# One paired DMA transpose split in two, and one exponential moved by a step, in a fused attention and feed-forward kernel on one core

## The chip, the cores and the metric

The kernel runs on 1 core of one Trainium2 chip. The metric is device time of one execution in microseconds (us), the median of several runs. TensorE (PE) multiplies matrices, VectorE (DVE), ScalarE (ACT) and GpSimd (POOL) work on elements, SyncE (SP) issues most DMAs.

## The reference

For each of 8 batches and 8 heads, 512 tokens `x` (width 64) and 32 states attend to each other; the 544 rows of every batch, 512 wide, then go through a feed-forward layer of width 2048 with a leaky ReLU.

```python
scores = scale * x @ state.T;   a  = softmax(scores);   xread = a @ state      # 512 rows per head
scores2 = scale * state @ x.T;  a2 = softmax(scores2);  sread = a2 @ x         # 32 rows per head
rows = concat([xread, sread])          # (8*544, 512) after the heads are joined
h = rows @ w_in;  g = maximum(0.01 * h, h);  out = g @ w_out
```

## The kernel before, in words

The batches run one behind the other. Each is an object `a` (`a0`, `a1`, `a2`, then `att_of[b]`), and its attention is prepared while the feed-forward of the batch before it keeps TensorE busy. The order of the instructions on every engine is the order in which the program writes them; engines wait for each other by semaphores alone.

The feed-forward of a batch is a loop of 16 steps `s`. Step `s` calls `ff1(a, hT, s)`: two matmuls into a PSUM bank `ph` (L428; there are two such banks, used in turn) and, on ScalarE, the leaky ReLU from that bank into `hT` (L433). Between the `ff1` of two steps stand products of the second layer (`piece`, `product`, `two_product`; tiles `py`, `ppx`, `ppb`, `ppr`) of this batch and of the one before, and the steps of the next batch's attention:

- `a_scores` (L256) fills the bank `sc` with scores of 32 states by 512 tokens, from `xT`, the tokens transposed by DMA (`a_xt_dma`, L234). `xT` comes from `xb`, the tokens cast by GpSimd (L132), and these from `xl`, loaded by SP (`load_x`, L99).
- `a_max`, `a_diff`, `a_exp` (ScalarE, L284), `a_recip`, `a_probs` give the first probabilities `aT`.
- `a_max2`, then `a_exp2(a, g)` for the two halves g = 0, 1 (ScalarE, L337, reading `sc`), then `a_probs2` (DVE, L345 to L355) give the second probabilities.
- The second probabilities are transposed by a DMA from SP: one by one (`a_a2t`, L362, of tile `a2`) for batches 2 to 5, in pairs (`a_a2t_pair`, L369, of tile `a2p`, which holds two batches) for batches 0 and 1 and for 6 and 7.
- `a_sread` (L380, PSUM tile `psr`, bank `big`) multiplies the transposed ones with `xb`; ScalarE copies the result to `sr_t` (L387). Its end also frees batch b's `xb` for a later batch.
- `a_m` (L407, tile `pm`) multiplies the states with `w_in` into `M`, a quarter at a time. At step 10 three of them stand in a row: into banks `ph` and `py` ("phpy"), into `big` and into `sc`.

The change touches two places. In the loop of batch 1 (L1053 to L1089), SP gets, in this order, `a_xt_dma` of batch 3 (step 7), `load_x(4)` (step 11), `a_a2t_pair(0)` (step 13), and then `a_a2t` of batch 2. In batch 2's loop `a_sread(a0)` stands in step 4 and `a_sread(a1)` in step 7, and batch 3's attention has `a_exp` in step 4, `a_exp2` in steps 6 and 8 (6 and 7 in later batches), and `a_probs` and `a_probs2` in step 8, with `a_m` in step 10.

Of the kernel before, what the change touches and what calls it, by code (L numbers as in the profile page):

```python
# [9 lines left out]
P = 128  # L10
# [5 lines left out]
NT = S // P  # L16
# [3 lines left out]
BF16 = mybir.dt.bfloat16  # L20
# [7 lines left out]
def kernel(  # L28
# [14 lines left out]
    att = ctx.enter_context(tc.tile_pool(name="att", bufs=2))  # L43
# [278 lines left out]
    def a_recip(a):  # L322
        a.q1b = block_recip(a.e1, NB)
# [18 lines left out]
    pairs = {}  # L342

    def a_probs2(a):
        nc.vector.tensor_scalar(out=a.r2[:], in0=a.r2[:], scalar1=1e-9, scalar2=None, op0=ALU.add)  # L345
        q2 = att.tile([P, 2], FP32, name="qc", tag="qc")
        nc.vector.reciprocal(q2[:], a.r2[:])
        if a.b in (0, 6):
            pairs[a.b] = att.tile([P, 2, 2, S], BF16, name="a2p", tag="a2p", bufs=1)
        if a.b in (0, 1, 6, 7):  # L350
            a.a2 = pairs[a.b - a.b % 2][:, a.b % 2]
        else:
            a.a2 = att.tile([P, 2, S], BF16, name="a2", tag="a2", bufs=1)[:]
        for g in range(2):
            nc.vector.tensor_scalar(  # L355
                out=a.a2[:, g, :], in0=a.e2[:, g, :],
                scalar1=q2[:, g:g + 1], scalar2=None, op0=ALU.mult,
            )
# [5 lines left out]
        )  # L364
        a.a2T = t[:]

    def a_a2t_pair(b):
        t = att.tile([P, 2, 2, NT, P], BF16, name="a2pT", tag="a2pT", bufs=1)
        nc.sync.dma_start_transpose(  # L369
            t[:].rearrange("p b g i q -> p (b g i) q"),  # L370
            pairs[b][:].rearrange("p b g s -> p (b g s)"),
        )
        for v in range(2):
            att_of[b + v].a2T = t[:, v]

    def a_sread(a):
        ps = psum.tile([P, NK, 2, NS], FP32, name="psr", tag="big", bufs=1)
# [379 lines left out]
    att_of = [Attn() for _ in range(B)]  # L757
# [148 lines left out]
    q = [recip0(0)]  # L906
# [62 lines left out]
    for j, tag in ((4, "ph"), (6, "big"), (8, "py"), (10, "big"), (12, "py"), (14, "ph")):  # L969
        t, bk = open_ff1_0(tag)  # L970
# [82 lines left out]
    for s in range(16):  # L1053
        ff1(a1, h1, s)
        if s % 2:
            pb, hT, i, jq = fill[s // 2]
            piece(pb, hT, i, jq)
        if s == 1:
            for n, j in ((3, 0), (3, 4), (4, 0)):
                tw_sum(n, j, j + 4, nc.vector)  # L1060
        elif s == 3:
            a_scores(a2)
            m_evict(a2, 0, a_m(a2, 0, "big"), SCA)
            a_shift(a2)
            a_max2(a2)
            tw_sum(4, 4, 8, nc.vector)
        elif s == 5:
            load_state(1)
        elif s == 7:
            a_exp(a2)  # L1070
            a_open(att_of[3], 3)
            a_xt_dma(att_of[3])
        elif s in (9, 11):
            a_exp2(a2, s // 2 - 4)
            if s == 9:
                a_recip(a2)
                a_probs(a2)
            else:
                a_probs2(a2)
                load_x(4, nc.sync)  # L1080
        elif s == 13:
            a_probs2(a1)
            a_a2t_pair(0)
            pm = [a_m(a2, 1, "big"), a_m(a2, 2, "sc")]
            m_evict(a2, 1, pm[0], VEC)
            m_evict(a2, 2, pm[1], SCA)
            q1 = two_open(h1, 2 * P, ("S0", "S1"), "py")
            for n in (1, 2, 3):
                two_sum(q1, n, 0, 4, nc.vector)  # L1089
# [3 lines left out]
    for b in range(2, B):  # L1093
        hT = hpool.tile([P, 16, S], BF16, name="hT", tag="hT")
        hTs[b] = hT
        a = att_of[b]
        nxt = att_of[b + 1] if b + 1 < B else None
        if b == 2:
            two_keep(q1, "S2")
            fill = {i: [lambda i=i: piece(1, h1, i, 3)] for i in range(2)}  # L1100
            for s, n in zip((2, 3, 5, 6, 8, 9, 11), (1, 2, 6, 5, 3, 7, 4)):
                fill[s] = [lambda n=n: two_product(q1, n)]
            fill[11].append(lambda: nc.sync.dma_start(pair_rows(1, 1), q1.y[:]))
        else:
            order = (2, 6, 5, 7, 3, 4)
            fill = {
                s: [lambda n=order[s // 2], v=s % 2: product(b - 1, n, v)] for s in range(12)
            }
            for i, n in enumerate(order):
                if n not in (2, 7):  # L1110
                    fill[2 * i + 1].append(lambda n=n: after(b - 1, n))
        fill[12 if b < 6 else 13] = [lambda: product(b, 1, 0)]
        fill[14] = [lambda: product(b, 1, 1, 0, 4)]
        fill[15] = [lambda: product(b, 1, 1, 4, 8), lambda: after(b, 1)]
        for s in range(16):
            ff1(a, hT, s)
            if s == 0:
                if b + 2 < B:
                    open_xb(b + 2)
                if b == 7:  # L1120
                    a_a2t_pair(6)
                elif b != 6:
                    a_a2t(a)
                for n in (1, 2) if b > 2 else (1, 2, 3):
                    if b > 2:
                        s_sum(b - 1, n, 4, 8, nc.vector)
                    else:
                        two_sum(q1, n, 4, 8, nc.vector)
            elif s == 1:
                if nxt is not None:  # L1130
                    a_scores(nxt)
                m_evict(a, 3, a_m(a, 3, "big"), SCA)
                if nxt is not None:
                    a_max(nxt)
                if b > 2:
                    for j in range(0, HJ, 2):
                        s_sum(b - 1, 4, j, j + 2, nc.gpsimd)
                else:
                    for j in (4, 0):
                        two_sum(q1, 4, j, j + 4, nc.gpsimd)  # L1140
                    state_cast(1, nc.gpsimd)
                if b + 2 < B:
                    cast_all(b + 2)
            elif s == 4:
                if b == 2:
                    state_t(1)
                    a_sread(a0)
            elif s == 7:
                if b == 2:
                    a_sread(a1)  # L1150
            elif s == 13:
                if b < 6:
                    a_sread(a)
            elif s == 10:
                if b == 7:
                    a_sread(att_of[6])
            elif s == 12:
                if b == 7:
                    a_sread(a)
                for n in (1, 2):  # L1160
                    s_sum(b, n, 0, 4, nc.vector)
                for j in (0, 4):
                    s_sum(b, 3, j, j + 4, nc.vector)
            if nxt is not None:
                if s == 4:
                    a_exp(nxt)
                elif s in ((6, 8) if b == 2 else (6, 7)):
                    if b == 2 and s == 6:
                        for f in fill.pop(6):
                            f()  # L1170
                    a_exp2(nxt, int(s > 6))
                if s == 7:
                    a_recip(nxt)
            if s == 9 and b + 2 < B:
                a_open(att_of[b + 2], b + 2)
                a_xt_dma(att_of[b + 2])
                if b + 3 < B:
                    load_x(b + 3, nc.sync)
            if b == 7:
                if s == 0:  # L1180
                    fa_open()
                elif s == 13:
                    fb_sums()
            for f in fill.get(s, ()):
                f()
            if b == 7 and s in FA_AT:
                i = FA_AT.index(s)
                fa_sum(i % 4 + 1, FJ * (i // 4), FJ * (i // 4 + 1))
            if s == 1:
                if b > 2:  # L1190
                    after(b - 1, 2)
                if nxt is not None:
                    a_diff(nxt)
                    if b > 2:
                        a_max2(nxt)
            elif s == 3 and b == 2:
                a_max2(nxt)
            elif s == (8 if b == 2 else 7):
                if b > 2:
                    after(b - 1, 7)  # L1200
                if nxt is not None:
                    a_probs(nxt)
                    a_probs2(nxt)
            elif s == 10 and nxt is not None:
                pm2 = a_m(nxt, 2, "phpy")
                pm0 = a_m(nxt, 0, "big")
                pm1 = a_m(nxt, 1, "sc")
                for g, copy in enumerate((SCA, VEC)):
                    copy(nxt.M[:, g, 2 * DM:3 * DM], pm2[g][:])
                m_evict(nxt, 0, pm0, VEC)  # L1210
                m_evict(nxt, 1, pm1, SCA)
# [3 lines left out]
    b = B - 1  # L1215
# [72 lines left out]
```

## Time and profile before

| | |
|---|---|
| time, median of 3 runs | 204.12 us (203.95 to 204.6) |
| the profiled execution's own time | 204.44 us |
| its span | 202.7 us |
| granted TensorE clock, mean | 0.998 |
| PE, DVE, ACT, POOL busy | 97%, 79%, 71%, 31% |

The profile is one execution, taken by the hardware profiler. Times in it count from the start of its span. L380 is line 380 of the kernel before. A row of a timeline gives the start, the time until the end of the last instruction that it joins, engine, line, operation, `out<-in`, sizes and count, and in brackets idle time before it with what ended it. "SPq" is SP's queue of issues: the time there is that of the issue, not of the transfer. In a list of waits the numbers are us in total, times, and the longest.

### The profile page before, as it was taken

The page shows a single profiled execution, that of the slowest core. Times are in us where ns is not written, and L with a number is a line of the kernel's source. Part 1 is how long each engine was busy: PE and PEld are TensorE (multiplying, and loading weights), DVE is VectorE, ACT ScalarE, POOL GpSimd, SP SyncE. Part 2 cuts the span into 40 slices and gives each one's busy share as a digit, 9 for nine tenths or more (in the row PEclk, how much of TensorE's full clock was granted, in tenths as well). Part 3 has the DMA queues.
Part 4 walks back from the last instruction along what each step waited for, and adds up shares of the span by engine and source line. Part 5 has one row for each costly group of instructions (what it writes and reads, how often), then busy time and mean ns, then how long its engine had stood idle before and what let it go on. Part 6 is the DMA issues. An engine that isn't in the chain of part 4 may idle for free.

```text
span 202.7 us, 4607 instructions
## 1 busy us (share of the span) xinstructions
PE 196.1 (97%) x1880; PEld 129.2 (64%) x1880; DVE 160.2 (79%) x242; ACT 144.3 (71%) x273; POOL 62.3 (31%) x67
## 2 busy tenths in 40 slices
PE   7979999999999999999999999999999999999993
PEld 2643534443467667766776677676767677799982
DVE  2865898899989999879996998699879935984712
ACT  3669777788979877778787779686958665757420
POOL 8734180030280274007600580054005600540000
PEclk9999999999999999999999999999999999999999
DMA  6999999697997726834194505220026202210115
GB/s 205 204 207 299 253 259 162 150 335 139 270 212 133 282 53 53 248 155 120 22 244 152 158 3 105 105 107 0 0 107 158 49 3 91 119 42 13 52 40 169
DMA packets 38741, 27.75 MB, mean 137 GB/s; under 512 B 24384, under 2 KB 35776, under 8 KB 38720
## 3 DMA queue, kind: packets, MB, share of 16 engines
q1 hardware_dynamic: 33552, 20.78, 40.3%
q0 software_dynamic: 4832, 6.29, 15.2%
q10 hardware_dynamic: 336, 0.39, 0.8%
q8 instruction: 14, 0.23, 0.5%
q14 instruction: 7, 0.06, 0.1%
HBM read 17.30 MB, written 8.91 MB: 129 GB/s over the span
## 4 chain that ended last, share of the span: by engine, by line
PE 76%; DMA 9%; DVE 7%; ACT 4%; POOL 1%; issue 1%; ACTq 1%; POOLq 0%
PE ph L428 18%; PE ppx L628 17%; PE ppb L628 15%; DMA w_in_bf<-in_moe_w_in_dram 5%; PE pyw L533 3%; PE ppr L685 3%; PE pm L407 3%; DMA a2pT<-a2p 3%; PE pf L506 3%; PE py L533 3%; PE ppw L628 3%; PE ph L933 2%; PE psr L380 2%; PE php L933 1%; DVE tw L572 1%; ACT hT L433 1%
## 5 line engine op out<-in xcount | busy, mean ns | idle before, releaser
L433 ACT ACTIVATE hT<-ph 128x512 bf16<-128x512 f32 x112 | 66.4, 603 | 24.0 <-PE ph L428 23.1
L428 PE MATMUL ph<-aT,M 128*128 128x512 bf16 x224 | 65.4, 380 | 0.1
L593 POOL TENSOR_TENSOR S<-hT,S 128x512 bf16<-128x512 bf16 x24 | 32.1, 1358 | 83.6 <-DVE S L593 65.5
L628 PEld LDWEIGHTS <-S 128*128 128x128 bf16 x384 | 37.3, 98 | 12.8
L628 PEld LDWEIGHTS <-hT 128*128 128x128 bf16 x288 | 27.6, 98 | 11.8 <-issue 1.9
L593 DVE TENSOR_TENSOR S<-hT 128x1024 bf16<-128x1024 bf16 x24 | 25.0, 1068 | 2.7 <-ACT hT L433 2.7
L428 PEld LDWEIGHTS <-M 128*128 128x128 bf16 x224 | 20.8, 98 | 9.5 <-issue 3.7
L628 PE MATMUL ppx<-tw,S 128*128 128x256 bf16 x160 | 20.7, 273 | 0.0
L533 PEld LDWEIGHTS <-hT 128*128 128x128 bf16 x96 | 9.0, 98 | 11.5 <-issue 1.3
L533 PE MATMUL py<-w_out_bf,hT 128*128 128x512 bf16 x64 | 16.0, 380 | 0.0
L421 ACT CAST M<-pm 128x1024 bf16<-128x1024 f32 x13 | 13.2, 1014 | 0.6 <-PE pm L407 0.6
L132 POOL CAST xb<-xl 128x2048 bf16<-128x2048 f32 x5 | 9.5, 1891 | 13.3 <-DMA xl<-in_x_dram 12.6
L725 DVE TENSOR_TENSOR ysb<-ppb,s 128x512 f32<-128x512 f32 x12 | 8.3, 692 | 5.5 <-PE ppb L628 5.5
L628 PE MATMUL ppb<-w_out_bf,hT 128*128 128x256 bf16 x96 | 12.5, 273 | 0.0
L628 PE MATMUL ppb<-tw,S 128*128 128x256 bf16 x96 | 12.4, 273 | 0.0
L628 PE MATMUL ppb<-w_out_bf,S 128*128 128x256 bf16 x96 | 12.3, 273 | 0.0
L628 PE MATMUL ppx<-w_out_bf,hT 128*128 128x256 bf16 x80 | 11.2, 273 | 0.0
L337 ACT ACTIVATE e<-sc,mcol 128x512 bf16<-128x512 f32 x16 | 11.1, 697 | 0.0
L289 DVE TRANSPOSE_TENSOR_REDUCE r<-e 128x32 f32<-128x1024 bf16 x7 | 8.7, 1245 | 2.9 <-ACT e L284 2.9
L628 PE MATMUL ppx<-tw,hT 128*128 128x256 bf16 x80 | 10.4, 273 | 0.0
L331 DVE TENSOR_REDUCE mcol<-sc 128x2 f32<-128x1024 f32 x8 | 9.7, 1214 | 0.0
L266 DVE TRANSPOSE_TENSOR_REDUCE mrow<-sc 128x32 f32<-128x1024 f32 x7 | 8.7, 1243 | 0.5 <-PE sc L256 0.5
(148 smaller groups left out, 311.5 us busy)
## 6 DMA issues: line engine op xcount, KB each, us to landing
out_dram<-ysb SPq DMA_DIRECT2D x11, 512.0 KB, 2.6
xl<-in_x_dram SPq DMA_DIRECT2D x5, 1024.0 KB, 6.6
out_dram<-ysb SPq DMA_DIRECT2D x9, 256.0 KB, 4.0
w_in_bf<-in_moe_w_in_dram POOLq DMA_DIRECT2D x4, 512.0 KB, 10.2
xf<-in_x_dram SPq DMA_DIRECT2D x4, 256.0 KB, 3.7
w_out_bf<-in_moe_w_out_dram POOLq DMA_DIRECT2D x4, 256.0 KB, 13.5
x<-in_x_dram POOLq DMA_DIRECT2D x2, 512.0 KB, 14.5
w_out_bf<-in_moe_w_out_dram POOLq DMA_DIRECT2D x2, 512.0 KB, 14.9
```

The costliest lines, as they stand in the source:

```text
L132: nc.gpsimd.tensor_copy(xt[b][:].rearrange("p t h d -> p h t d"), xl[b][:].rearrange("p h (t d) -> p h t d", t=NT),)
L266: nc.vector.tensor_reduce(out=m1[:], in_=flat.rearrange("p (c j) -> p c j", j=NS), axis=AX.X, op=ALU.max, apply_transpose=True,)
L289: nc.vector.tensor_reduce(out=r1[:], in_=e1[:].rearrange("p (c j) -> p c j", j=NS), axis=AX.X, op=ALU.add, apply_transpose=True,)
L331: nc.vector.tensor_reduce(out=a.m2[:], in_=a.sc[:], axis=AX.X, op=ALU.max, negate=True)
L337: nc.scalar.activation(out=a.e2[:, g], in_=a.sc[:, g, :], func=AF.Exp, bias=a.m2[:, g:g + 1], accum_out=a.r2[:, g:g + 1],)
L421: copy(a.M[:, :, cols], pm[:])
L428: nc.tensor.matmul(ph[:], lhsT=a.M[:, g, P * j:P * (j + 1)], rhs=a.aT[:, g, :], start=(g == 0), stop=(g == 1),)
L433: nc.scalar.activation(out=hT[:, j, :], in_=ph[:], func=AF.Prelu, scale=1 / SCALE, alpha=0.01)
L533: nc.tensor.matmul(y.py, lhsT=hT[:, j, P * i:P * (i + 1)], rhs=w_out_bf[:, j, :], start=(j == 0), stop=(j == 15),)
L593: eng.tensor_tensor(out=part(n), in0=in0, in1=in1, op=op)
L628: nc.tensor.matmul(q[bank][v], lhsT=lhsT, rhs=w_of(n, j), start=q["open", bank] and j == 0, stop=j == 7, skip_group_check=True,)
L725: nc.vector.tensor_tensor(out=to, in0=of, in1=in1, op=ALU.add)
```

## The change

`a_a2t_pair` gets a list of the batches of the pair to transpose, and is called twice for the first pair: for batch 0 in step 9 of batch 1's loop, ahead of `load_x(4)` on SP, and for batch 1 in step 13, where the whole pair's call stood. Each call transposes 8 blocks of 128 x 128 instead of 16. In batch 2's loop the second half of `a_exp2` of batch 3 goes from step 8 to step 9, so that ScalarE's `hT` of step 9 comes ahead of it, and `a_probs2` follows it, behind the DVE sum of product 7 that stands in step 9. The other batches and the pair 6 and 7 stay as they are.

```diff
-    def a_a2t_pair(b):
-        t = att.tile([P, 2, 2, NT, P], BF16, name="a2pT", tag="a2pT", bufs=1)
+    pairs_t = {}
+
+    def a_a2t_pair(b, vs=(0, 1)):
+        if b not in pairs_t:
+            pairs_t[b] = att.tile([P, 2, 2, NT, P], BF16, name="a2pT", tag="a2pT", bufs=1)
+        lo, hi = vs[0], vs[-1] + 1
         nc.sync.dma_start_transpose(
-            t[:].rearrange("p b g i q -> p (b g i) q"),
-            pairs[b][:].rearrange("p b g s -> p (b g s)"),
-        )
-        for v in range(2):
-            att_of[b + v].a2T = t[:, v]
+            pairs_t[b][:, lo:hi].rearrange("p b g i q -> p (b g i) q"),
+            pairs[b][:, lo:hi].rearrange("p b g s -> p (b g s)"),
+        )
+        for v in vs:
+            att_of[b + v].a2T = pairs_t[b][:, v]
...
             if s == 9:
+                a_a2t_pair(0, (0,))
                 a_recip(a2)
                 a_probs(a2)
...
         elif s == 13:
             a_probs2(a1)
-            a_a2t_pair(0)
+            a_a2t_pair(0, (1,))
...
-                elif s in ((6, 8) if b == 2 else (6, 7)):
+                elif s in ((6, 9) if b == 2 else (6, 7)):
...
                 if nxt is not None:
                     a_probs(nxt)
-                    a_probs2(nxt)
+                    if b > 2:
+                        a_probs2(nxt)
+            elif s == 9 and b == 2:
+                a_probs2(nxt)
```

## The prediction

> **What bounds the kernel now.** I read the page first, then busy time by stage, the chain of waits between 57 and 77 us, and the timelines of PE, SP, ACT, DVE and POOL around the edited steps. From the page: the span and the engines' busy time.
>
> ```profile
> span 202.7 us, 4607 instructions
> PE 196.1 (97%) x1880; PEld 129.2 (64%) x1880; DVE 160.2 (79%) x242; ACT 144.3 (71%) x273; POOL 62.3 (31%) x67
> ```
>
> TensorE sets the time; only what keeps it idle can be won. The busy table by stretch (PE, PEld, DVE, ACT, POOL, then clock, DMA share, GB/s) says where that is:
>
> ```profile
> 58.00:66.00 8.00, 7.52 (x86) 5.40 (x93) 6.69 (x13) 7.36 (x18) 2.31 (x2) 1.00 0.85 187
> 66.00:190.00 124.00, 124.00 (x1222) 90.39 (x1207) 103.47 (x141) 92.00 (x173) 37.60 (x27) 1.00 0.34 97
> ```
>
> From 66 to 190 us PE never stops, at full granted clock, while DVE, ACT and POOL have room: what PE gains before 66 reaches the end of the kernel. From 58 to 66 it loses 8.00 - 7.52 = 0.48 us, in batch 2's loop, which the change edits. The wait there:
>
> ```profile
> PEld L380 <- DMA a2pT<-a2p: 0.9, 1, 0.9
> ```
>
> PE stands before batch 0's `a_sread` (`psr`) until the transpose of the pair (`a2pT`) has landed. PE's timeline shows that stop and a second one:
>
> ```profile
> 57.51 0.59 PE L428 MATMUL ph<-aT,M 128*128 128x512 bf16 x2
> 58.46 0.64 PE L380 MATMUL psr<-a2pT,xb 128*128 128x64 bf16 x16 [0.36 <-DMA a2pT<-a2p]
> ...
> 61.55 0.59 PE L428 MATMUL ph<-aT,M 128*128 128x512 bf16 x2
> 61.98 0.63 PE L380 MATMUL psr<-a2pT,xb 128*128 128x64 bf16 x16
> ...
> 65.06 0.60 PE L428 MATMUL ph<-aT,M 128*128 128x512 bf16 x2
> 65.77 0.84 PE L407 MATMUL pm<-w_in_bf,st_t 64*32 64x512 bf16 x24
> 66.54 0.61 PE L428 MATMUL ph<-aT,M 128*128 128x512 bf16 x2
> ...
> 73.11 0.59 PE L428 MATMUL ph<-aT,M 128*128 128x512 bf16 x2
> 73.63 0.41 PE L256 MATMUL sc<-xT,st_t 64*32 64x512 bf16 x8
> ```
>
> Busy ends are modelled, so I go by starts. An `ff1` (`ph`) followed at once by `psr` takes 61.98 - 61.55 = 0.43 us; at 57.51 it takes 0.95. Lost: 0.52. An `ff1` followed by matmuls of the other tile shape takes 73.63 - 73.11 = 0.52 where nothing waits; at 65.06 it takes 0.71. Lost: 0.19. The second stop's cause is in the chain:
>
> ```profile
> 51.45 6.97 DMA a2pT<-a2p
> ...
> 65.23 0.50 ACT hT L433
> 65.73 0.04 issue
> 65.77 0.37 PE pm L407
> ```
>
> Step 10's `a_m(nxt, 2, "phpy")` takes the `ph` bank of step 9, and ScalarE empties it late.
>
> **The transpose in two.** SP before:
>
> ```profile
> 46.58 1.72 SPq L234 DMA_TRANSPOSE xT<-xb  x1
> 48.41 1.16 SPq L99 DMA_DIRECT2D xl<-in_x_dram  x1
> 51.45 3.41 SPq L369 DMA_TRANSPOSE a2pT<-a2p  x1
> 54.91 1.30 SPq L362 DMA_TRANSPOSE a2T<-a  x1
> ```
>
> Removed: one transpose of 16 blocks, which waited for batch 1's probabilities (`a2p`, written at 50.81 by DVE, below). Added: two of 8 blocks. The first needs only batch 0's probabilities (37.94), so it issues when SP is done with batch 3's `xT`, at about 48.4. What 8 blocks cost SP is bounded by 1.30 (`a2T`, the same shape) and 1.71 (half of 3.41); I take 1.7, the dearer. It is queued ahead of `load_x(4)`, which goes from 48.41 to about 50.1 and issues until 51.3; the second half then goes at about 51.45, no later than the pair did. `a2T` of batch 2 moves from 54.91 to about 53.2.
>
> ```profile
> DMA to landing us min/median/max: 6.6/6.6/6.6
> 37.94 0.62 DVE L355 TENSOR_SCALAR a2p<-e,qc 128x512 bf16<-128x512 bf16 x2
> 50.81 0.62 DVE L355 TENSOR_SCALAR a2p<-e,qc 128x512 bf16<-128x512 bf16 x2
> 56.91 1.50 POOL L209 TENSOR_SCALAR stb<-stf 128x512 bf16<-128x512 f32 x1
> 59.17 1.89 POOL L132 CAST xb<-xl 128x2048 bf16<-128x2048 f32 x1 [0.75 <-PE psr L380]
> ```
>
> The first of these lines is `xl` of batch 4: it landed 6.6 after 48.41, at 55.0. The first half lands by at most 6.97 after its issue (what the whole pair took), 55.4, where PE now wants it at 57.51 + 0.43 = 57.94: 2.5 us of cover. So 0.52 goes. `load_x(4)`, 1.7 later, lands at 56.7; POOL can't cast it before `stb` ends at 58.41 and `psr` has freed the buffer (58.6): hidden with 1.7 to spare, and the cast itself comes 0.5 earlier, `a_xt_dma(4)` behind it too. The second half is queued behind that load; the pair landed 58.41 - 55.0 = 3.4 after the load before it, so half of it lands 1.7 to 3.4 after 56.7, at 58.4 to 60.1. Batch 1's `psr` will want it at 61.98 - 0.52 = 61.46: hidden by 1.4 us or more; without that cover each us later costs PE a us. `a2T` of batch 2 has until 69 us.
>
> The Trainium skill, "DMA: Bandwidth & Descriptors", section "Rules for kernel authors", says the reverse of this edit: join small transfers into one large one, since small ones are mostly overhead. The rows speak against it here: two issues of 1.30 are less than the one of 3.41. The same page of the Trainium skill, section "Latency and other measured facts", gives about 2 us of fixed cost for a DMA; as an estimate from that page the second half would land at 60.4 to 62.1, and the gain at the first `psr` would be given back at the second by up to 0.6.
>
> **The exponential a step later.** ScalarE before:
>
> ```profile
> 59.14 0.53 ACT L387 CAST sr_t<-psr 64x128 bf16<-64x128 f32 x2 [0.40 <-PE psr L380]
> 59.69 1.06 ACT L284 ACTIVATE e<-sh 128x1024 bf16<-128x1024 f32 x1
> ...
> 63.97 0.60 ACT L433 ACTIVATE hT<-ph 128x512 bf16<-128x512 f32 x1
> 64.46 0.68 ACT L337 ACTIVATE e<-sc,mcol 128x512 bf16<-128x512 f32 x1
> 65.03 0.20 ACT L337 ACTIVATION_READ_ACCUMULATOR e<-sc,mcol 128x1 f32 x1
> 65.12 1.16 ACT L433 ACTIVATE hT<-ph 128x512 bf16<-128x512 f32 x2
> ```
>
> ScalarE runs back to back here, and its chain starts at `sr_t`, which follows `psr`. So with `psr` 0.52 earlier the chain moves along: step 8's `hT` goes from 63.97 to 63.45. Now `hT` of step 9 follows (63.94, spacing 64.46 - 63.97 = 0.49, ended at 64.54), then the exponential (64.43), then `hT` of step 10 (0.66 after it, 65.12 - 64.46; not before its `ff1`, 64.54 + 0.60 = 65.14; so 65.16 to 65.76). PE's step 10 goes from 65.06 to 64.54, and `pm` wants the bank at 64.54 + 0.52 = 65.06: it was emptied at 64.54, so the 0.19 goes too, and `pm` starts at 65.06 instead of 65.77.
>
> What is late next? The diff adds one wait on PE: the last of the three `a_m` of step 10 takes the bank `sc`, which the moved exponential now frees later. It comes two thirds through `pm`'s 0.77 (66.54 - 65.77), at 65.57; the exponential ends at 64.43 + 0.68 = 65.11, its accumulator's read at about 65.2: 0.4 us of cover; behind that wait PE holds `ff1` of step 11 and all that follows. And `ff1` of step 11 at 65.06 + 0.77 = 65.83 needs step 10's `hT`, ended at 65.76 plus 0.04: cover 0.03, so up to 0.2 may come back here (the read of the accumulator, if it isn't hidden). On DVE, `a_probs2(nxt)` moves behind the sum of product 7:
>
> ```profile
> 66.20 0.42 DVE L695 TENSOR_TENSOR ysb<-ppr,rkept 128x256 f32<-128x256 f32 x1
> ```
>
> That sum is no longer queued behind the exponential's scalings and comes earlier; the copies of `M` still come behind the two scalings, at worst where they are; this `M` is first read by PE in the next batch's step 0, five steps on. Nothing.
>
> **The sum.** 0.52 + 0.19 = 0.71. The profiled execution took 204.44 (span 202.7 and 1.7 around it) and would take 203.73, span 202.0. Against the median of the runs, 204.12, that is 203.41, 0.35% less. About 0.3%, 0.6 us, is what a measurement of this kernel tells from no change, and the sum stands just beyond it.
>
> **Rivals.**
> 1. ScalarE takes part back. In its stretch it is busy 7.36 of 8, so what PE gains it may lose 0.1 to 0.5 later, at `ff1` of step 11 or at the bank `sc`: 203.5 to 203.9. For: the 0.03 of cover. Against: steps 5 to 9 keep their distances when the chain moves as a whole.
> 2. The edit does nothing at `psr`: the first half doesn't get ahead (queued behind other packets) and PE stops as before; then the 0.19 alone is won, 203.9, or nothing, 204.1. Against: 2.5 us of cover.
> 3. Slower: each 8-block transpose holds the queue for all its time to landing and not only for its issue. `a2T` lands 4.2 after its issue:
>
> ```profile
> DMA to landing us min/median/max: 4.2/4.2/4.2
> ```
>
>  Then the first half holds it from 48.4 to 52.6, `xl` lands at 59.2, the second half at 63.4, and batch 1's `psr` waits 63.4 - 61.46 = 1.9: 204.12 - 0.71 + 1.9 = 205.3. It decides from a landing at 61.46 + 0.71 = 62.2. The rule of the Trainium skill on joining transfers, named above, speaks for this one. Against: the pair and `a2T` landed at 58.4 and 59.1, less than a us apart, so transposes overlap in the queue (58.4 is 51.45 + 6.97, 59.1 is 54.91 + 4.2).
>
> **How the numbers follow.** Both stops gone, 203.41 give or take 0.3 for the runs' own spread: chance 0.62, of which 0.5 beyond 0.3%. Rival 1: 0.18, a fifth of it still beyond 0.3%. Rival 2: 0.08. Rival 3: 0.12. So faster 0.54, same 0.34, slower 0.12. The range is 203.1 to 204.2: the forecast with the spread, rivals 1 and 2; what lies outside is rival 3 and a little below.
>
> **Right or wrong in the changed profile.** Right: no wait of PE for `a2pT`; the first `psr` starts at 57.9 and `pm` of step 10 at 65.1; the first transpose at 48.4 on SP, `xl` right behind it; batch 3 to 7 as before, 0.7 earlier. Wrong: a wait for `a2pT` at the second `psr` (rival 3), PE idle before `ff1` of step 11 or in `pm` with ACT as its releaser (rival 1), or a first `psr` still at 58.4 (rival 2).

## The result, and the profile after

| | before | changed |
|---|---|---|
| median of 16 runs each, us | 204.13 (203.61 to 204.72) | 203.39 (202.9 to 204.24) |
| ratio to before | | 0.9963, 95% interval 0.995 to 0.9976 |
| profiled execution, us | 204.44, span 202.7 | 203.53, span 201.6 |

Faster by 0.37%, 0.74 us; forecast were 0.35% and 0.71. Line numbers after are 4 to 8 higher than before (`ff1`'s matmuls are L432, its leaky ReLU L437, `psr` L384, `pm` L411). The profile after holds 27 fewer records of matmuls than the one before, so I read starts and not sums. Two of the profiles further down (tw_pool and batch1_early) are of executions whose first 20 us ran at a granted clock of 0.91 and ended 2.8 us late; from these I use distances inside the later loops alone, and such executions (two of six of batch1_early) count in the medians below but not in the ratios.

PE's timeline after (start, time, engine, line, operation, tiles), the two places of the prediction's stops:

```profile
57.26 0.38 PE L432 MATMUL ph<-aT,M 128*128 128x512 bf16 x1
57.69 0.63 PE L384 MATMUL psr<-a2pT,xb 128*128 128x64 bf16 x16
...
64.28 0.59 PE L432 MATMUL ph<-aT,M 128*128 128x512 bf16 x2
64.80 0.84 PE L411 MATMUL pm<-w_in_bf,st_t 64*32 64x512 bf16 x24
65.57 0.60 PE L432 MATMUL ph<-aT,M 128*128 128x512 bf16 x2
```

`psr` follows its `ff1` by 57.69 - 57.26 = 0.43 (0.95 before) and `pm` by 0.52 (0.71 before); `ff1` of step 11 follows `pm` by 0.77, as before. Nothing waits for the first pair's `a2pT` any more. The span is shorter by more than the sum of the two: this execution was 0.25 ahead before the edit could act (57.51 to 57.26 at the `ff1` of step 4), and 0.97 ahead behind it (66.54 to 65.57). The difference, 0.72, is the edit's, and it reaches the end.

SP's queue of issues after, and below it the landings of the two halves (shortest, median, longest) and of batch 4's tokens:

```profile
48.47 1.83 SPq L373 DMA_TRANSPOSE a2pT<-a2p  x1
50.40 0.52 SPq L99 DMA_DIRECT2D xl<-in_x_dram  x1
51.52 1.67 SPq L373 DMA_TRANSPOSE a2pT<-a2p  x1
53.24 3.20 SPq L362 DMA_TRANSPOSE a2T<-a  x1
```

```profile
DMA to landing us min/median/max: 3.7/5.6/7.4
```

```profile
DMA to landing us min/median/max: 6.2/6.2/6.2
```

The first half lands 3.7 after 48.47, at 52.2, long before 57.69. The tokens land at 56.6, 1.6 later than before, and the second half 7.4 after 51.52, at 58.9; its `psr` starts at 61.20.

ScalarE after:

```profile
58.38 0.52 ACT L391 CAST sr_t<-psr 64x128 bf16<-64x128 f32 x2
58.93 1.06 ACT L284 ACTIVATE e<-sh 128x1024 bf16<-128x1024 f32 x1
...
63.22 1.09 ACT L437 ACTIVATE hT<-ph 128x512 bf16<-128x512 f32 x2
64.19 0.69 ACT L337 ACTIVATE e<-sc,mcol 128x512 bf16<-128x512 f32 x1
64.91 0.60 ACT L437 ACTIVATE hT<-ph 128x512 bf16<-128x512 f32 x1
```

The `hT` of steps 8 and 9 now run together (the row of 63.22 joins both), the exponential comes behind them, and step 10's `hT` ends at 65.51, just ahead of the `ff1` at 65.57 that needs its bank.

### The profile page after: what moved, and what is told of

It is laid out like the page before. It is cut to its first block, busy times and chain, and to the rows that moved or that the text cites. A ratio compares the mean times of both kernels' runs of the same rounds, so it can differ in the third digit from the quotient of the medians.

```text
span 201.6 us, 4587 instructions
## 1 busy us (share of the span) xinstructions
PE 194.7 (97%) x1853; PEld 129.6 (64%) x1880; DVE 160.1 (79%) x242; ACT 144.2 (72%) x273; POOL 62.5 (31%) x67
## 4 chain that ended last, share of the span: by engine, by line
PE 76%; DMA 14%; DVE 3%; POOL 2%; ACT 1%; issue 1%; ACTq 1%; POOLq 0%
PE ph L432 20%; PE ppx L632 18%; PE ppb L632 15%; DMA w_out_bf<-in_moe_w_out_dram 8%; PE ppr L689 6%; DMA w_in_bf<-in_moe_w_in_dram 5%; PE py L537 3%; PE pf L510 3%; PE pm L411 3%; PE ppw L632 3%; PE psr L384 2%; PE pyw L537 2%; PE sc L256 1%; POOL w_in_bf L145 1%; DVE tw L576 1%
## 5 line engine op out<-in xcount | busy, mean ns | idle before, releaser
L437 ACT ACTIVATE hT<-ph 128x512 bf16<-128x512 f32 x112 | 66.4, 604 | 23.6 <-PE ph L432 19.5
L432 PE MATMUL ph<-aT,M 128*128 128x512 bf16 x201 | 60.5, 379 | 0.2
L432 PEld LDWEIGHTS <-M 128*128 128x128 bf16 x224 | 20.8, 98 | 9.4 <-issue 3.7
```

What stands on the lines that cost most here:

```text
L432: nc.tensor.matmul(ph[:], lhsT=a.M[:, g, P * j:P * (j + 1)], rhs=a.aT[:, g, :], start=(g == 0), stop=(g == 1),)
L437: nc.scalar.activation(out=hT[:, j, :], in_=ph[:], func=AF.Prelu, scale=1 / SCALE, alpha=0.01)
```

## The experiments

My theory was that the two stops are separate: the first is the transpose's landing behind batch 4's load, the second the exponential's place on ScalarE. The rival was that the second only hands on the first, since ScalarE's chain starts at `psr`. Ratios below are to the kernel before in the same series, with their 95% intervals.

| kernel | median, us | ratio | interval |
|---|---|---|---|
| split_only | 203.42 | 0.9971 | 0.9954 to 0.9987 |
| split_again | 203.4 | 0.9969 | 0.9949 to 0.999 |
| exp_only | 203.85 | 0.9989 | 0.9972 to 1.0005 |
| exp_two_later | 204.28 | 1.0005 | 0.999 to 1.0021 |
| pair_ahead | 203.55 | 0.9967 | 0.9955 to 0.998 |
| halves_behind | 203.14 | 0.996 | 0.9939 to 0.9981 |
| changed kernel (after_again) | 203.1 | 0.9955 | 0.9936 to 0.9973 |
| changed kernel (after_third) | 203.23 | 0.9954 | 0.994 to 0.9969 |
| batch1_exp | 203.07 | 0.9949 | 0.9929 to 0.997 |
| tw_pool | 203.21 | 0.997 | 0.9958 to 0.9981 |
| batch1_tw | 203.84 | 0.9998 | 0.9974 to 1.0021 |
| batch1_early | 202.76 | 0.9928 | 0.9912 to 0.9944 |

### One part alone: split_only, split_again, exp_only

split_only takes back the exponential's move; exp_only takes back the split.

```diff
# split_only, split_again
-                elif s in ((6, 9) if b == 2 else (6, 7)):
+                elif s in ((6, 8) if b == 2 else (6, 7)):
# and a_probs2(nxt) back behind a_probs(nxt) in step 8
# exp_only
-                a_a2t_pair(0, (0,))
...
-            a_a2t_pair(0, (1,))
+            a_a2t_pair(0)
```

> Only the transpose in two, batch 0's half ahead of batch 4's tokens; the exponential stays in step 8. My theory (two independent stops of TensorE, of 0.52 and 0.19 us): no wait for a2pT, the first psr follows its ff1 by 0.43 us, but step 10's pm still follows its ff1 by 0.71, because the exponential still stands ahead of step 9's hT on ScalarE: 0.52 less than before, 203.6. The rival (the second stop is only the first one handed on by ScalarE, whose chain starts at psr): pm follows by 0.52 and the whole 0.71 to 0.75 is won here, 203.4.

> The split alone once more, since its first profile had VectorE 0.5 us late against TensorE (tw at 44.63 took 1.43 to the next start instead of 0.60, with GpSimd's cast beside it). My theory: with VectorE undisturbed the first stop is gone and step 10's pm starts 6.08 after the start of a_exp, as before, so it still follows its ff1 by 0.71 to 0.75: 0.52 less than before, 203.5 to 203.6. The rival (the second stop only hands on the first): pm follows by 0.52.

> Only the exponential in step 9 with its scalings behind it; the pair is transposed by one DMA as before. My theory: psr still follows its ff1 by about 0.95 us (the pair lands at about 58.4), pm follows its ff1 by 0.52: 0.19 less than before, 203.9, within what a measurement tells from no change. The rival (the second stop is only the first one handed on): nothing is won, pm still follows by 0.7.

In split_only's profile the first stop was gone (`psr` 0.43 after its `ff1`), but 0.15 was lost before `ff1` of step 7, and ScalarE's `a_exp` had waited 0.28 for VectorE's `sh`. `pm` followed its `ff1` by 0.84 there, more than the 0.71 expected, with ScalarE's `hT` as the releaser. The disturbance comes from further up and is taken up below; it is the reason for running this kernel again. PE in split_again:

```profile
57.67 0.38 PE L432 MATMUL ph<-aT,M 128*128 128x512 bf16 x1
58.10 0.63 PE L384 MATMUL psr<-a2pT,xb 128*128 128x64 bf16 x16
...
64.68 0.59 PE L432 MATMUL ph<-aT,M 128*128 128x512 bf16 x2
65.42 0.84 PE L411 MATMUL pm<-w_in_bf,st_t 64*32 64x512 bf16 x24
```

And in exp_only:

```profile
57.15 0.59 PE L432 MATMUL ph<-aT,M 128*128 128x512 bf16 x2
58.02 0.64 PE L384 MATMUL psr<-a2pT,xb 128*128 128x64 bf16 x16 [0.28 <-DMA a2pT<-a2p]
...
64.62 0.59 PE L432 MATMUL ph<-aT,M 128*128 128x512 bf16 x2
65.14 0.84 PE L411 MATMUL pm<-w_in_bf,st_t 64*32 64x512 bf16 x24
```

With the split alone (split_again) `psr` follows by 0.43 and `pm` still by 0.74; with the exponential alone `psr` follows by 0.87 and `pm` by 0.52. Each part removes its own stop and leaves the other: the rival falls. The times have the forecast sizes (0.6 and 0.2 less), but exp_only's interval takes in 1, and between the split alone and the whole change, 0.1 to 0.2%, the intervals overlap; there the starts decide, not the times.

### The price of the added wait: exp_two_later

```diff
-                elif s in ((6, 9) if b == 2 else (6, 7)):
+                elif s in ((6, 10) if b == 2 else (6, 7)):
...
-            elif s == 9 and b == 2:
-                a_probs2(nxt)
             elif s == 10 and nxt is not None:
+                if b == 2:
+                    a_probs2(nxt)
```

> The changed kernel with the exponential one step later still, in step 10, behind step 10's hT and ahead of the three pm. It prices the wait that the change added, on the bank sc. My theory: the exponential then ends about 66.1 (times of the profile after), the third pm wants the bank at 65.3: TensorE stops for 0.7 to 0.8 us in pm, released by ScalarE, and nearly all of the gain is gone: 204.1. If the bank sc were free otherwise, or TensorE ran on: no change from the changed kernel, 203.4.

```profile
64.71 0.63 PE L411 MATMUL pm<-w_in_bf,st_t 64*32 64x512 bf16 x16
66.13 0.41 PE L411 MATMUL pm<-w_in_bf,st_t 64*32 64x512 bf16 x8 [0.80 <-ACT e L337]
```

As expected: the third `pm` stands 0.80 until the exponential has read the bank `sc`. `ff1` of step 11 starts at 66.47, 1.76 after `pm` instead of 0.77, so 0.99 is lost, and the kernel is back at the time of before. Of the three steps tried, step 9 is the one between two stops: in step 8 the exponential delays step 9's `hT`, in step 10 it holds `sc`. An earlier step, such as the 7 of the later batches, was not tried.

### Is it the split, or the place in the queue: pair_ahead, halves_behind

```diff
# pair_ahead: one DMA for the pair, batch 4's tokens loaded behind it
-                a_a2t_pair(0, (0,))
...
-                load_x(4, nc.sync)
...
-            a_a2t_pair(0, (1,))
+            a_a2t_pair(0)
+            load_x(4, nc.sync)
# halves_behind: both halves in step 13, behind batch 4's tokens
-                a_a2t_pair(0, (0,))
...
+            a_a2t_pair(0, (0,))
             a_a2t_pair(0, (1,))
```

> The exponential in step 9; the pair in one DMA, but batch 4's tokens are loaded behind it instead of ahead of it. If the pair was late because it stood in the queue behind the load, it lands about 5 us after its issue at 51.4, at 56.5, before the 57.9 that TensorE wants, and the result is that of the changed kernel (0.71 less than before, 203.4); the tokens land by about 61.5, their cast comes 2 to 3 us later, and scores of batch 4 at 73 do not wait. If the size of the transpose itself made it late (7.0 from issue to landing), it still lands at 58.4, the first stop of 0.52 stays, and only 0.19 is won (203.9).

> The changed kernel, but both halves are issued in step 13, behind batch 4's tokens. If it is the load ahead in the queue that makes the transpose late, the first half now lands 2 to 3 us after the load, at about 57.0 to 57.6, just ahead of the 57.7 that TensorE wants or up to 0.2 after it: 203.4 to 203.6. If halving alone were what counts, it would land at 51.4 + 3 = 54.5, and nothing would differ from the changed kernel. If neither helps, it lands at 58.4 as the pair did, and 0.5 us of stop is back.

Both runs keep the exponential in step 9. SP, the pair's landing, then PE, in pair_ahead:

```profile
51.08 2.02 SPq L373 DMA_TRANSPOSE a2pT<-a2p  x1
53.20 0.86 SPq L99 DMA_DIRECT2D xl<-in_x_dram  x1
54.11 3.01 SPq L362 DMA_TRANSPOSE a2T<-a  x1
```

```profile
DMA to landing us min/median/max: 4.8/4.8/4.8
```

```profile
57.14 0.59 PE L432 MATMUL ph<-aT,M 128*128 128x512 bf16 x2
57.58 0.63 PE L384 MATMUL psr<-a2pT,xb 128*128 128x64 bf16 x16
```

And in halves_behind (the row of 49.64 joins both halves; the second was issued at 51.9):

```profile
48.48 1.07 SPq L99 DMA_DIRECT2D xl<-in_x_dram  x1
49.64 5.28 SPq L373 DMA_TRANSPOSE a2pT<-a2p  x2
```

```profile
DMA to landing us min/median/max: 6.3/6.4/6.4
```

```profile
57.91 0.38 PE L432 MATMUL ph<-aT,M 128*128 128x512 bf16 x1
58.34 0.63 PE L384 MATMUL psr<-a2pT,xb 128*128 128x64 bf16 x16
```

In both `psr` follows by 0.43 or 0.44, so neither the split nor the place ahead of the load is needed by itself. The whole pair is in time when the load goes behind it: it lands 4.8 after its issue, at 55.9, instead of 7.0. The load pays for that: batch 4's tokens land 6.8 after 53.20, at 60.0, and GpSimd's cast of them starts at 60.11 instead of 58.45, which delayed nothing on TensorE. Behind the load, the first half lands 6.3 after its issue, at 55.9 too, ahead of the 57.7 at which the changed kernel's `psr` starts. It is in time because it no longer waits for batch 1's probabilities and can issue at 49.64 instead of 51.45; the second half, issued at 51.9, lands at 58.3, like the whole pair before. I had given the first half the old issue time in that expectation, which was wrong.

### What comes next: the changed kernel again, tw_pool, and three attempts in batch 1's loop

> The changed kernel again, beside the others of this call. My theory: psr follows its ff1 by 0.43, pm by 0.52, as in its first profile; 0.71 less than before on the same chip, 203.3 to 203.4. What the first profile left open: whether VectorE's a_diff (sh) ends ahead of ScalarE's need for it (there 58.59 against sr_t's end at 58.90). Where GpSimd's cast of batch 3's tokens starts late and holds up VectorE's tw at 44 to 46, sh ends later; from 0.3 us of that, ff1 of step 7 begins to wait.

> The changed kernel, to stand beside the other of this call. 0.7 less than before on the same chip if VectorE is undisturbed, down to 0.6 if GpSimd's cast of batch 3's tokens holds up tw at 44 to 46 (then up to 0.1 of stop before ff1 of step 7 and 0.03 before step 11).

after_third repeats the first profile (0.43, 0.52, 0.78). after_again doesn't quite. PE, and ScalarE's `a_exp`:

```profile
59.41 1.04 PE L689 MATMUL ppr<-tw,Sr 128*128 128x256 bf16 x8
60.37 0.59 PE L432 MATMUL ph<-aT,M 128*128 128x512 bf16 x2
```

```profile
58.63 1.06 ACT L284 ACTIVATE e<-sh 128x1024 bf16<-128x1024 f32 x1 [0.21 <-DVE sh L280]
```

`ff1` of step 7 follows its product by 0.96, where 0.87 is the distance without a wait (59.89 to 60.76 in after_third): 0.09 is lost, since `a_exp` waits 0.21 for `sh`. The chain behind `sh` begins with a sum that VectorE makes at 44 to 46 (`tw`, L572 and L576), beside GpSimd's cast of batch 3's tokens. In the kernel before and in after_again:

```profile
45.11 0.68 DVE L572 TENSOR_TENSOR tw<-w_out_bf,tw 128x1024 bf16<-128x1024 bf16 x1
```

```profile
43.19 1.89 POOL L132 CAST xb<-xl 128x2048 bf16<-128x2048 f32 x1 [12.56 <-DMA xl<-in_x_dram]
```

```profile
44.38 1.45 DVE L576 TENSOR_TENSOR tw<-w_out_bf,tw 128x1024 bf16<-128x1024 bf16 x1
```

```profile
43.39 1.89 POOL L132 CAST xb<-xl 128x2048 bf16<-128x2048 f32 x1 [13.11 <-DMA xl<-in_x_dram]
```

Before, the cast ended at 45.08 and the sum ran behind it in 0.68. In after_again the cast ended at 45.28, the sum was due at 44.38 and took 1.45. `a_exp`'s wait follows the sum's length in the profiles of the changed kernel and of the split alone: none at 1.01, 1.25 and 1.30, 0.21 at 1.45, 0.28 at 1.51 (split_only). From this came two theories to try: take the sum off VectorE (tw_pool), and go after the next stop, 0.25 us and some 0.06 in batch 1's loop, where ScalarE's `a_exp` of batch 2 waits for `sh` with step 8's `hT` behind it (batch1_exp, then with the sum on GpSimd, then with the sum made before the cast).

```diff
# tw_pool, against the changed kernel
-            tw_sum(4, 4, 8, nc.vector)
+            for j in (4, 6):
+                tw_sum(4, j, j + 2, nc.gpsimd)
# batch1_exp, against the changed kernel: a_exp(a2) from step 7 to 9, both a_exp2(a2) in step 11
         elif s == 7:
-            a_exp(a2)
...
         elif s in (9, 11):
-            a_exp2(a2, s // 2 - 4)
             if s == 9:
+                a_exp(a2)
                 a_a2t_pair(0, (0,))
+                a_probs2(a1)
                 a_recip(a2)
                 a_probs(a2)
             else:
+                a_exp2(a2, 0)
+                a_exp2(a2, 1)
                 a_probs2(a2)
...
         elif s == 13:
-            a_probs2(a1)
# batch1_tw: batch1_exp with the sum on GpSimd, as in tw_pool
# batch1_early, against batch1_exp: the sum in step 1, on VectorE
-            for n, j in ((3, 0), (3, 4), (4, 0)):
+            for n, j in ((3, 0), (3, 4), (4, 0), (4, 4)):
...
-            tw_sum(4, 4, 8, nc.vector)
```

> The changed kernel with one sum of w_out blocks, the one that VectorE makes at 44 to 46 (tw 4, second half), given to GpSimd as two instructions behind its cast of batch 3's tokens. It tests what I think comes next: the sum is held up by that cast in some executions, VectorE's chain to batch 3's a_diff then ends after ScalarE wants it, and TensorE stops up to 0.1 us before ff1 of step 7. My theory: VectorE's reciprocal of batch 2 starts at once behind max2, a_diff ends 0.6 to 1.2 earlier, ff1 of step 7 never waits; 0.1 less than the changed kernel at most, so 203.0 to 203.1, no more than the runs can tell. The rival: GpSimd's two instructions hold up VectorE's or their own followers instead, and a_diff is no earlier.

> An attempt to go on from the changed kernel, one loop earlier: in batch 1's loop TensorE still loses about 0.3 us before ff1 of steps 10 and 11 (45.5 in the profile after), because ScalarE's a_exp of batch 2 waits for VectorE's sh with step 8's hT behind it. Here a_exp goes from step 7 to step 9, behind that hT, both halves of a_exp2 to step 11, and batch 1's scalings come ahead of batch 2's reciprocal to fill VectorE's wait. My theory: the stop at 45.5 goes and nothing else comes late: 0.3 less than the changed kernel, 203.1. The rival: VectorE, which is full from 46 to 59, becomes later, a_exp of batch 3 waits for sh, and ff1 of step 7 in the next loop stops for what was won: 203.4.

> The earlier attempt in batch 1's loop (a_exp of batch 2 two steps later) with the same sum given to GpSimd. That attempt took away the stop of 0.31 at 45.5 and lost 0.25 of it again before ff1 of step 7 and 0.03 before step 11, because a_diff of batch 3 came late on VectorE. My theory: with the sum off VectorE the 0.31 stays won: TensorE's starts after 66 us 0.3 earlier against its own start of batch 1's loop than in the changed kernel, 202.8. The rival: another row of the full VectorE takes its place, and the time stays at 203.1.

> The attempt in batch 1's loop (a_exp of batch 2 in step 9, both halves of a_exp2 in step 11, batch 1's scalings ahead of batch 2's reciprocal), with the sum tw 4, second half, staying on VectorE but made in step 1 beside the others, before GpSimd's cast begins. My theory: a_exp's new place has 0.8 us of room for sh to come 0.6 later; no sum meets the cast; VectorE's chain to batch 3's a_diff ends about 0.7 earlier than in the first attempt, ff1 of step 7 and step 11 no longer wait, and the 0.31 at 45.5 stays won: 0.3 less than the changed kernel, 1.0 less than before. The rival, from the two attempts before this one: another row takes its place and the time is that of the changed kernel.

tw_pool is no faster than the changed kernel; its `sh` ended 0.4 after `psr`'s start instead of 0.9, so the cover (the time by which an input is early) grew, and nothing was there to win in its profile. For batch1_exp and the others, the place of the stop first in the changed kernel, then in batch1_exp:

```profile
44.38 1.03 PE L537 MATMUL py<-w_out_bf,hT 128*128 128x512 bf16 x4
45.50 1.08 PE L432 MATMUL ph<-aT,M 128*128 128x512 bf16 x4
```

```profile
44.05 1.03 PE L537 MATMUL py<-w_out_bf,hT 128*128 128x512 bf16 x4
44.92 1.03 PE L432 MATMUL ph<-aT,M 128*128 128x512 bf16 x4
...
59.26 1.04 PE L689 MATMUL ppr<-tw,Sr 128*128 128x256 bf16 x8
60.37 0.59 PE L432 MATMUL ph<-aT,M 128*128 128x512 bf16 x2
```

The stop goes (0.87 instead of 1.12), and `ff1` of step 7 in the next loop gives 0.24 of it back (1.11 instead of 0.87): the rival of that run was right, and the time is the changed kernel's. With the sum on GpSimd (batch1_tw) the stop was gone too, and 0.19 of it came back before `ff1` of step 7, now with VectorE's scalings held up by GpSimd's sum. Its median was 0.6 us above that profile and level with the kernel before, and why stays open. With the sum made early (batch1_early):

```profile
47.21 1.03 PE L537 MATMUL py<-w_out_bf,hT 128*128 128x512 bf16 x4
48.08 1.03 PE L432 MATMUL ph<-aT,M 128*128 128x512 bf16 x4
...
62.41 1.04 PE L689 MATMUL ppr<-tw,Sr 128*128 128x256 bf16 x8
63.29 0.59 PE L432 MATMUL ph<-aT,M 128*128 128x512 bf16 x2
```

The distances are 0.87 and 0.88: the stop is gone and stays gone. The ratio is 0.9928, against 0.9954 for the changed kernel in the same series; the intervals just overlap. The starts account for some 0.3 us of that difference of 0.5; with few executions of it, this is the fastest version here but not shown to be so beyond the noise.

## Why the prediction was right, point by point

- **The first stop, 0.52.** Gone, and by the split: split_again has it without the exponential's move. The landings came as worked out: tokens at 56.6 (forecast 56.7), second half at 58.9 (58.4 to 60.1), 8 blocks 1.83 and 1.67 of SP's time (1.7). The first half landed sooner than its bound, 52.2 against 55.4. The place in the queue was not the only cure, though, as pair_ahead and halves_behind show.
- **The second stop, 0.19.** Gone, and by the exponential: exp_only has it without the split. That the two add up without eating each other held.
- **The sum.** 0.71 forecast, 0.72 between the starts of the two profiles, 0.74 between the medians. That these agree to a few hundredths is luck: the first stop was 0.44 in exp_only's profile, and the second 0.22 and 0.32 in the two profiles of the split alone, so the parts vary by 0.1 from one execution to another. It was right to carry the sum to the end undiminished: TensorE is 0.97 ahead at 65.6 and, with that, 1.1 ahead at the end of the span.
- **The covers.** The 0.4 before the bank `sc` held, and exp_two_later shows what lies behind it. The 0.03 before `ff1` of step 11 held in two of the three profiles of the changed kernel, and cost 0.04 in after_again.
- **What the working left out.** Rival 1 looked for ScalarE's delay at step 11 and at `sc`. The cover that wears out first is one that I had not listed: VectorE's `sh`, which `a_exp` of step 4 needs. Before, it was ready 1.2 ahead of `a_exp`'s start (57.29 + 1.23, against 59.69); after, 0.34 ahead (57.36 + 1.23, against 58.93), and in after_again it was late. Of that loss `psr` earlier is 0.5, and 0.33 is the sum's meeting with the cast, which took it from 0.68 to 1.01 in the profile after too. The late `sh` cost the changed kernel 0.09 in after_again; in batch1_exp it took 0.24 of a further gain of 0.25.
- **Rival 3, and the rule on joining transfers.** Transposes overlapped in the queue: the second half landed at 58.9, not at 63.4. The Trainium skill ("DMA: Bandwidth & Descriptors", "Rules for kernel authors") advises one large transfer instead of many small ones and calls those under 64 KB mostly overhead; each half here is 256 KB, so the rule hardly bears on this edit. Two halves and one whole, each well placed, gave the same time (0.996 and 0.9967), so the split neither paid nor cost by itself. The prediction's own reason against the rule, two issues of 1.30 against one of 3.41, did not hold: the halves took SP 1.83 and 1.67, 3.50 together; the sum had used 1.7 each, so it lost nothing. The same page of the Trainium skill ("Latency and other measured facts") gives about 2 us of fixed cost for a DMA. It did not show as time that a second transfer adds, since the second half landed at 58.9 and not at 60.4 or later; whether it is part of each transfer's own time, 3.7 at least, no run here shows.

## What to carry to other kernels

When a transfer is late, ask first what it waits for and what stands ahead of it in its queue: moving the load behind it, or cutting off the part that waits for nothing, cured it alike here. Before adding up stops that a change removes, list for each instruction on the new path every input and how early it is, the ones that had plenty of room too; a gain moves the path towards them, and the next stop is the one whose cover is smallest then. An exponential or copy that reads a bank has its place between the step whose bank it delays and the step that takes its own bank: of the three steps tried here only one was free of both.

## What the runs showed of the hardware that I had not expected

VectorE's sum of 1024 columns took 0.68 where GpSimd's cast was over, and 1.45 where the cast ran for its first 0.9 us. In all six profiles where the cast ran 0.4 us or more into the sum, the sum took 1.01 to 1.51 and ended 0.54 or 0.55 after the cast; so it did not run slower but stood until the cast was over. The Trainium skill, "SBUF — State Buffer", section "SBUF: two separate sides", states that a GpSimd instruction that reads SBUF and a VectorE instruction with two inputs in SBUF, as this sum has, share a pair of ports under an exclusive lock that the first to come holds for its whole instruction; the rows agree. Whether they meet here goes with when a load lands in each execution. They met in six of the seven profiles that have the early half and the sum in its old place, and in none of the four without the early half; the halves are issued only after 47 us, and whether the edit has a part in it stays open.

SP's time to issue a transpose does not follow from its size alone: 16 blocks took 3.41 before and 2.02 in pair_ahead, and `a2T`'s 8 blocks took 1.30 before and 3.20 after, when the issues ahead of it were shorter. I did not find what sets it; none of it was on the path here.
